# Values' product of a talking-heads attention: three bursts a half become twelve parts tied to visits

## The chip, the cores and the metric

The kernel runs on one core of a Trainium2 chip. The metric is the device time of that core in microseconds (us). The matrix engine is called PE here (its weight loads PEld), the vector engine DVE, the activation engine ACT, the general-purpose engine POOL; SP issues the DMAs.

## The reference

Attention with four batches, twelve heads, 448 rows and 64 elements a head, whose scores and whose softmax are both mixed over the heads, and two MLPs behind it:

```python
scores = scale * np.matmul(q, k.transpose(0, 1, 3, 2))
scores = np.einsum('bhij,hg->bgij', scores, w_pre)
attn = softmax(scores)                       # over j
attn = np.einsum('bhij,hg->bgij', attn, w_post)
x = np.matmul(attn, v)                       # heads side by side: 1792 x 768
h = x @ w_in;  x = (h * np.cos(h)) @ w_out   # 2048 wide
h = np.maximum(np.maximum(x @ w1, x @ w2), x @ w3)
return h @ w_out2
```

All of it is float32.

## The kernel before, in words

The rows of a batch are cut into *chunks* of 10, 11 or 12 *slots* of ten rows. For each chunk and each head pair `qk` (line 545) makes the scores in PSUM, `evac` copies them to SBUF and `send` (line 564) brings them by DMA into a grid in which the partitions hold rows and heads together; there are two grids. A *visit* is two slots of a chunk, 92 in all. For each visit `mix1` (line 568) mixes the scores over the heads, `rowmax`, `soft`, `guard`, `recip` and `wscale` do the softmax on DVE and ACT, `mix2` (line 606) mixes the result over the heads into PSUM banks of the pool `ps_t`, one for each slot, and `keep` (line 619) copies each of them into the tile `a2`.

One or two chunks form a *half* (`HALVES`, line 26; four batches of two halves of 220 and 230 columns). When all visits of a half are kept, `av` (line 631) multiplies them with the values: three steps a half, each of two head pairs, each of these a bank of `ps_t` and 16 matmuls in 8 groups, recorded as 32 in a step. `keepx` (line 643) copies each head pair's result out, one copy for each chunk, and `out` writes it to `xT` in HBM, from which the MLPs read.

Everything is put in order before the launch by a planner (`Plan`, line 372). Each step has a rank, a time on each engine that may do it, steps that it needs (`after`), steps that must be issued first (`behind`) and places that it takes and frees; the planner plays the engines through and issues the steps in the order that comes out, in which each engine then runs its queue. A rank counts blocks, two for each visit. The steps of the change stand at lines 675 to 725. The ranks of the first MLP work hang on `r0` (line 891), the start of the last chunk; `open_early` (line 914) needs the sends of the last chunk, `xget` (line 936) the outputs of a batch and a grid's place, and `open_late` (line 975) the last `keepx`.

PSUM has eight banks: three for `mix1` (`ps_m`), three of `ps_t`, two for `qk` (`ps_x`), which go to the MLPs later.

Of the kernel before, what the change touches and what calls it, by code (L numbers as in the profile page):

```python
# [9 lines left out]
F32 = mybir.dt.float32  # L10
# [6 lines left out]
B, H, S, D = 4, 12, 448, 64  # L17
# [4 lines left out]
RI = 10  # L22
JB, JC = 4, 112
IBLK = [(0, S)]
QG = 1
HALVES = [[[10, 12], [12, 11]]] * B
NHALF = 230
RT = 12
RH = RI // 2
BUFS = {"k": 10, "q": 9, "s": 8, "e": 5, "w2s": 3, "v": 7, "xs": 6, "a2": 2, "ps_m": 3, "ps_t": 3, "ps_x": 2}  # L30

RANK = {"fwget": 3.598, "fw": 2.0, "fwgap": 2.0, "fx": 3.474, "fxgap": 0.827, "x1": 2.568, "fh": 7.0, "fhgap": 0.483, "fa": 12.527}
WAIT = 0.034
# [410 lines left out]
def attention(ctx, tc, q, k, v, w_pre, w_post, same_row, xT, tp, mlps):  # L444
    nc = tc.nc
    scores_only = ctx.enter_context(ExitStack())
    pool = lambda n, b: ctx.enter_context(tc.tile_pool(name=n, bufs=b))
    psum = lambda n, b: ctx.enter_context(tc.tile_pool(name=n, bufs=b, space=bass.MemoryType.PSUM))
# [2 lines left out]
    ep, wp, st, const, vp, xp, ap_ = (  # L451
        pool("e", BUFS["e"]), pool("w2s", BUFS["w2s"]), pool("st", 8), pool("const", 1),
        pool("v", 1), pool("xs", BUFS["xs"]), pool("a2", BUFS["a2"]))
    ps_m, ps_t = (psum(n, BUFS[n]) for n in ("ps_m", "ps_t"))
    ps_x = scores_only.enter_context(
        tc.tile_pool(name="ps_x", bufs=BUFS["ps_x"], side="right", space=bass.MemoryType.PSUM))
    q = q.rearrange("(b c e i) -> b c e i", b=B, c=H // 2, e=4 * D)
# [22 lines left out]
    score, halves = [], []  # L480
    for b, sizes in enumerate(HALVES):
        i = 0
        for n, half in enumerate(sizes):
            start, column = i, 0
            for slots in half:
                i = min(i, S - RI * slots)
                score.append((b, i, RI * slots, slots, 2 * b + n, column))
# [140 lines left out]
    def pairs(x):  # L628
        return 2 * x, 2 * x + 1

    def av(half, x, _):
        b, _, _, m, _ = halves[half]
        a2 = live["a2", half]
        for hp in pairs(x):
            vt = live["v", b, hp]
            live["av", hp] = ps_t.tile([128, JB, H, RI], F32, name="aps")
            ps = live["av", hp] = live["av", hp].rearrange("p j g i -> p (j g i)")
            for j in range(JB):
                for g in range(2):
                    nc.tensor.matmul(ps[64 * g:64 * g + 64, :m], vt[:, j, g, :], a2[:, j, 2 * hp + g, :m],  # L640
                                     start=j == 0, stop=j == JB - 1)

    def keepx(half, hp, eng):

# [11 lines left out]

    before = {}

    def add(f, a, rank, engines, after=(), turn=False, **kw):

        key = f.__name__, *a
        plan.add(key, rank, partial(f, *a), engines, after, behind=before.get(f, ()) if turn else (), **kw)
        if turn:
            before[f] = [key]

    HP = H // 2


    for x in range(3):
# [5 lines left out]
    for n in range(NS):  # L675
        b = score[n][0]
        start, end = score[n - 1][0] != b or not n, n == NS - 1 or score[n + 1][0] != b
        for hp in range(HP):
            r = (first[n - 1] + 0.5 + 0.125 * score[n - 1][3] * hp) if n else -40.0 + hp
            if start:  # L680
                early = 8.0 if b else 20.0
                add(qget, (b, hp), r - early, {"D": 0.6}, turn=True, takes=["q"], lands=2.5)
                add(kget, (b, hp), r - early, {"D": 0.6}, turn=True, takes=["k"], lands=2.5)
            ring = score_bank(n, hp)[0]
            add(qk, (n, hp), r, {"T": 0.8}, [("qget", b, hp), ("kget", b, hp)], turn=True, takes=[ring] * 2,
                frees=[(f, (f + "get", b, hp)) for f in "kq"] if end else [])
            for h in range(2 * hp, 2 * hp + 2):
                add(evac, (n, h), r, {"A": 0.55, "V": 0.62}, [("qk", n, hp)], turn=True, takes=[place := copy_place(n, h)[0]], frees=[(ring, ("qk", n, hp), h % 2)])
                if h == 0:
                    plan.add(("new_t", n), r, lambda _: None, {}, [("evac", n, 0)], takes=["t"])  # L690
                add(send, (n, h), r, {"D": score[n][2] / 118.0}, [("evac", n, h), ("new_t", n)], turn=True, frees=[(place, ("evac", n, h))], lands=2.5)


    for y, (n, t, slots) in enumerate(visits):
        i = 2 * y
        key = lambda f, *x: (f, y, *x)
        add(mix1, (y,), i, {"T": 0.8}, [("wmix", 0), ("fill", n % 2)] + [("send", n, h) for h in range(H)], turn=True, takes=["ps_m"] * 2,
            frees=[("t", ("new_t", n))])
        for a in range(2):
# [6 lines left out]
            frees=[("e", key("soft", a)) for a in range(2)] + [("w2s", key("wscale"))])  # L706
        for c in slots:
            begin = n == halves[score[n][4]][4][0] and t == c == 0
            add(keep, (y, c), i + 1.5, {"A": 0.57, "V": 0.65}, [key("mix2")], turn=True, takes=["a2"] * begin,
                frees=[("ps_t", key("mix2"), c)])  # L710


    for half, (b, _, _, _, members) in enumerate(halves):
        last = (first + [N])[members[-1] + 1] - 1
        ends = [("keep", y, a) for y, x in enumerate(visits) if x[0] in members for a in x[2]]
        start = ends[0]
        for x in range(HP // 2):
            r = last + 2.5 + 3.0 * x
            for hp in pairs(x) if half % 2 == 0 else ():
                add(vget, (b, hp), r - 10.0, {"D": 0.8}, [("send", 0, H - 1)], turn=True, takes=["v"], lands=3.0)  # L720
            add(av, (half, x), r, {"T": 3.25}, [("vget", b, hp) for hp in pairs(x)] + ends, turn=True, takes=["ps_t"] * 2,
                frees=[("a2", start)] + [("v", ("vget", b, hp)) for hp in pairs(x) if half % 2])
            for hp in pairs(x):
                add(keepx, (half, hp), r, {"A": 0.45, "V": 0.5}, [("av", half, x)], turn=True, takes=["xs"], frees=[("ps_t", ("av", half, x), hp % 2)])
                add(out, (half, hp), r, {"D": 0.5}, [("keepx", half, hp)], turn=True, frees=[("xs", ("keepx", half, hp))], lands=3.0)


# [190 lines left out]
    for r, job in sorted(jobs):  # L918
        early = job[0] == "w" and job[1] < FG + 1
        if early:  # L920
            after = [("open_early",)]
# [11 lines left out]
        free(hold[0], ("convert", job, 6))  # L933
    for n in range(2):
        r = (r0, N - 1)[n] + RANK[("fx", "x1")[n]]
        add(xget, (n,), r, {"D": 3.6}, [("out", 2 * n + x, hp) for x in range(2) for hp in range(H // 2)] + [("xget", 0)] * n
            + [("block", FG)], takes=["t"])
        for c in range(KC):
            add(xhi, (n, c), r + 2.0 + c * RANK["fxgap"], {"A": 0.467}, [("xget", n)])
            add(xlo, (n, c), r + 2.0 + c * RANK["fxgap"], {"P": 1.09, "V": 0.535}, [("xhi", n, c)])  # L940
# [96 lines left out]
    for s in range(1, NSTEP):  # L1037
        if s == NSTEP - 1:
# [20 lines left out]
             behind=[("token", ("high", x, 0)) for x in ("11", "21", "T1", "T2", "T3", "T4")])  # L1059
# [35 lines left out]
    for u, (l, (j, wi)) in enumerate(units):  # L1095
# [8 lines left out]
        for i, (name, (eng, _, needs)) in enumerate(live["U", u][1].items()):  # L1104
            kind, x = name
# [109 lines left out]
```

## Time and profile before

| | |
|---|---|
| median of three runs | 1170.45 us (1168.78 to 1172.11) |
| the profiled execution | 1172.04 us |
| its span, first to last instruction | 1170.3 us |
| granted clock of PE, mean | 0.996 of full speed |
| attention, first mix1 to the last product's end | 23.3 to 387.9 us |

The profile is of one execution. Busy time of an engine is the time in which the profile shows an instruction in it; PE's matmuls are pipelined and their ends are modelled, so that PE can show as busy while it waits. A float32 matmul of the attention is recorded as two. The costs of PE work are therefore best read from start to start of groups that follow each other.

### The profile page before, as it was taken

To read this page: it belongs to the slowest core of one execution; us is meant where nothing else is said; L and a number is where in the kernel's file an instruction comes from. 1 tells how busy PE (TensorE), PEld (TensorE's weight loads), DVE (VectorE), ACT (ScalarE), POOL (GpSimd) and SP (SyncE) were. 2 spreads that over 40 slices of the span, in tenths; PEclk is the share of its full clock that TensorE was granted. 3 is DMA by queue.
4 is the path that set the end of the run, shared out by engine and by line. 5 is a ranking of instruction groups with operands and counts; after the bars stand their busy time and mean duration, and the time that the engine had idled before them with its cause. 6 is when DMAs were issued, how large, how long until landed. Compare 5 with 4: busy or idle time off the path is not lost.

```text
span 1170.3 us, 29431 instructions
## 1 busy us (share of the span) xinstructions
PE 1130.7 (97%) x11836; PEld 926.5 (79%) x11836; DVE 992.9 (85%) x2083; ACT 656.3 (56%) x1468; POOL 79.8 (7%) x69
## 2 busy tenths in 40 slices
PE   7899999899898899999999999999999999999998
PEld 2566566565556699999999999999999999999987
DVE  5878777777778899999999999997788679778994
ACT  3656556655657687555555555555534354445472
POOL 4000000000005110000000000000001021011110
PEclk9999999999999999999999999999999999999999
DMA  6785565645553655343434344431002221222233
GB/s 220 226 242 163 169 195 158 185 132 153 155 170 116 213 155 149 115 136 115 135 115 135 115 135 121 130 108 34 1 28 82 61 67 35 76 66 69 82 117 113
DMA packets 90696, 146.02 MB, mean 125 GB/s; under 512 B 8928, under 2 KB 73536, under 8 KB 90560
## 3 DMA queue, kind: packets, MB, share of 16 engines
q1 hardware_dynamic: 90304, 144.12, 40.8%
q8 instruction: 93, 1.52, 0.5%
q14 instruction: 43, 0.35, 0.1%
q0 software_dynamic: 256, 0.02, 0.0%
HBM read 84.96 MB, written 20.45 MB: 90 GB/s over the span
## 4 chain that ended last, share of the span: by engine, by line
PE 84%; DMA 6%; DVE 5%; issue 1%; ACT 1%; SPq 1%; ACTq 0%; DVEq 0%
PE ps L156 21%; PE ps L158 21%; PE ps L157 21%; PE mps L575 6%; PE aps L640 5%; PE aps L616 5%; PE ps L552 4%; DMA t<-s 3%; DMA x<-xT 1%; DVE nm L583 1%; DMA v<-in_v_dram 1%; DVE s L460 1%; DMA wraw<-in_w_in_dram 0%; ACT e L589 0%; DVE a L460 0%
## 5 line engine op out<-in xcount | busy, mean ns | idle before, releaser
L158 PE MATMUL ps<-x,w 128*128 128x448 f32 x816 | 300.0, 368 | 2.4 <-DVE x L147 1.5
L156 PE MATMUL ps<-x,w 128*128 128x448 f32 x816 | 300.4, 368 | 0.8 <-ACT gh L857 0.6
L157 PE MATMUL ps<-x,w 128*128 128x448 f32 x816 | 299.8, 367 | 0.5 <-DVE w L296 0.3
L156 PEld LDWEIGHTS ps<-x,w 128*128 128x128 f32 x816 | 153.7, 188 | 17.6 <-issue 2.4
L158 PEld LDWEIGHTS ps<-x,w 128*128 128x128 f32 x816 | 153.6, 188 | 17.4 <-POOL x L147 2.0
L157 PEld LDWEIGHTS ps<-x,w 128*128 128x128 f32 x816 | 153.7, 188 | 14.8 <-POOL w L131 0.8
L589 ACT ACTIVATE e<-mps,nm 128x448 f32<-128x448 f32 (+1 forms) x184 | 116.9, 637 | 79.2 <-DVE nm L583 59.3
L616 PEld LDWEIGHTS aps<-w2s,e 60*64 60x64 f32 x5760 | 108.7, 136 | 51.2 <-issue 23.8
L156 PE MATMUL ps<-gh,w 128*128 128x448 f32 x384 | 140.9, 367 | 0.0
L157 PE MATMUL ps<-gh,w 128*128 128x448 f32 x384 | 140.7, 366 | 0.0
L158 PE MATMUL ps<-gl,w 128*128 128x448 f32 x384 | 140.4, 366 | 0.0
L583 DVE TENSOR_REDUCE nm<-mps 128x1 f32<-128x448 f32 (+1 forms) x184 | 110.2, 616 | 30.8 <-PE mps L575 29.3
L293 ACT CAST w<-wf 128x384 fp32r<-128x384 f32 x168 | 81.1, 514 | 74.5 <-DVE wf L285 54.2
L616 PE MATMUL aps<-w2s,e 60*64 60x60 f32 x5760 | 112.7, 220 | 8.9 <-DVE w2s L603 6.2
L575 PE MATMUL mps<-t,w 64*64 64x448 f32 (+1 forms) x720 | 106.4, 558 | 10.2 <-DMA t<-s 6.2
L552 PE MATMUL ps<-k,q 64*64 64x448 f32 (+3 forms) x736 | 99.0, 551 | 5.1 <-ACT s L460 2.5
L814 DVE TENSOR_TENSOR acc<-ps,acc 128x448 f32<-128x448 f32 x168 | 100.2, 615 | 1.4 <-PE ps L158 1.4
L252 ACT ACTIVATE wf<-wraw 128x384 f32<-128x384 f32 x112 | 61.9, 553 | 51.3 <-DMA wraw<-in_w_out_dram 37.7
L296 DVE TENSOR_TENSOR w<-wf,w 128x384 fp32r<-128x384 f32 x132 | 73.7, 579 | 19.1 <-ACT w L293 18.3
L296 POOL TENSOR_TENSOR w<-wf,w 128x384 fp32r<-128x384 f32 x36 | 42.1, 1177 | 684.6 <-DVE wt L256 371.8
L640 PE MATMUL aps<-a,v 128*64 128x220 f32 (+1 forms) x768 | 78.0, 356 | 4.7 <-ACT xs L460 3.2
L640 PEld LDWEIGHTS aps<-a,v 128*64 128x64 f32 x768 | 54.2, 136 | 34.2 <-issue 5.9
(121 smaller groups left out, 1736.7 us busy)
## 6 DMA issues: line engine op xcount, KB each, us to landing
t<-s SPq DMA_DIRECT2D x96, 210.0 KB
wf<-w SPq DMA_DIRECT2D x96, 192.0 KB
wraw<-in_w_out_dram SPq DMA_DIRECT2D x44, 384.0 KB
wraw<-in_w_dram SPq DMA_DIRECT2D x36, 384.0 KB
wraw<-in_w_in_dram SPq DMA_DIRECT2D x32, 384.0 KB
t<-s SPq DMA_DIRECT2D x48, 192.5 KB
w<-wf SPq DMA_DIRECT2D x48, 192.0 KB
t<-s SPq DMA_DIRECT2D x43, 175.0 KB
```

The lines of the kernel that those rows point to most:

```text
L156: mm(w[0], x[0], start=first, stop=False)
L157: mm(w[1], x[0], start=False, stop=False)
L158: mm(w[0], x[1], start=False, stop=last)
L293: return nc.scalar.copy(A[x][0], w())
L296: return eng.tensor_sub(A[x][1], w(), f32(A[x][0]))
L552: nc.tensor.matmul(live["s", n, 2 * hp + g][r:end], live["q", b, hp][half, i0 + r:i0 + end], live["k", b, hp][half], start=True, stop=True)
L575: nc.tensor.matmul(live["m", v, a][64 * y:64 * y + 64], w1[k], grids[n % 2][k, t + y, :], start=True, stop=True)
L583: nc.vector.tensor_reduce(nm, of(v, live["m", v, a]), axis=AX.X, op=ALU.max, negate=True)
L589: nc.scalar.activation(of(v, e), of(v, live["m", v, a]), AF.Exp, bias=live["nm", v, a], scale=1.0, accum_out=live["z", v][:, a:a + 1])
L616: nc.tensor.matmul(live["a", v, y][64 * c:64 * c + 64, j, :, a, :], live["e", v, a][k, o:o + 64], live["w2s", v][k, a], start=True, stop=True)
L640: nc.tensor.matmul(ps[64 * g:64 * g + 64, :m], vt[:, j, g, :], a2[:, j, 2 * hp + g, :m], start=j == 0, stop=j == JB - 1)
L814: return nc.vector.tensor_add(acc, po, acc) if fg else nc.scalar.copy(acc, po)
```

## The change

`HALVES` gets a list for each batch: the first batch has halves of one chunk of 10 slots, one of 12, and two of 12 and 11; the last batch has 12 and 11, then 12, then 10 slots; the other two stay. The lists' chunks are in a new order in the last batch, and a half's number is counted as the halves are made.

`ps_t` has two banks instead of three, and a pool `ps_v` of one bank takes both head pairs of a step of `av`, side by side. A step of `av` becomes four parts: for each of the two head pairs, chunks 0 and 1 of the four in which the keys lie, then chunks 2 and 3, 4 matmuls each (8 recorded). The twelve parts of a half are issued behind the `mix1` of visits: the first behind that of the second visit after the half's last one, the rest spread over as many visits as the next half has, at most twelve. Parts whose visit would lie behind the last one are not tied. `keepx` follows the last part of its own head pair. `qk` of a chunk is issued behind `mix1` of a visit of the chunk before, from two visits ahead of that chunk's start for the first two head pairs to two visits into it for the sixth.

Values are loaded for the half that starts a batch, as before, and freed by the half that ends one; `xget` needs the outputs of all halves of its batch.

```diff
-HALVES = [[[10, 12], [12, 11]]] * B
+HALVES = [[[10], [12], [12, 11]], [[10, 12], [12, 11]], [[10, 12], [12, 11]], [[12, 11], [12], [10]]]
-BUFS = {..., "ps_m": 3, "ps_t": 3, "ps_x": 2}
+BUFS = {..., "ps_m": 3, "ps_t": 2, "ps_v": 1, "ps_x": 2}
...
-    def av(half, x, _):
+    def av(half, x, y, _):
         b, _, _, m, _ = halves[half]
         a2 = live["a2", half]
-        for hp in pairs(x):
-            vt = live["v", b, hp]
-            live["av", hp] = ps_t.tile([128, JB, H, RI], F32, name="aps")
-            ps = live["av", hp] = live["av", hp].rearrange("p j g i -> p (j g i)")
-            for j in range(JB):
-                for g in range(2):
-                    nc.tensor.matmul(ps[64 * g:64 * g + 64, :m], vt[:, j, g, :], a2[:, j, 2 * hp + g, :m],
-                                     start=j == 0, stop=j == JB - 1)
+        if y == 0:
+            both = ps_v.tile([128, 2 * NHALF], F32, name="avps")
+            for n, hp in enumerate(pairs(x)):
+                live["av", hp] = both[:, n * NHALF:(n + 1) * NHALF]
+        hp = pairs(x)[y // 2]
+        for j in range(2 * (y % 2), 2 * (y % 2) + 2):
+            for g in range(2):
+                nc.tensor.matmul(live["av", hp][64 * g:64 * g + 64, :m], live["v", b, hp][:, j, g, :], a2[:, j, 2 * hp + g, :m],
+                                 start=j == 0, stop=j == JB - 1)
...
+    starts = [next(y for y, x in enumerate(visits) if x[0] == n) for n in range(NS)] + [len(visits)]
+
+    def from_visit(y):
+        return [("mix1", y)] if 0 <= y < len(visits) else []
...
             add(qk, (n, hp), r, {"T": 0.8}, [("qget", b, hp), ("kget", b, hp)], turn=True, takes=[ring] * 2,
+                behind=from_visit(starts[n - 1] - 2 + max(hp - 1, 0)) if n > 1 else [],
                 frees=[(f, (f + "get", b, hp)) for f in "kq"] if end else [])
...
+        ylast = starts[members[-1] + 1] - 1
+        room = min(12, starts[halves[half + 1][4][-1] + 1] - 1 - ylast) if half + 1 < len(halves) else 12
...
-            add(av, (half, x), r, {"T": 3.25}, [("vget", b, hp) for hp in pairs(x)] + ends, turn=True, takes=["ps_t"] * 2,
-                frees=[("a2", start)] + [("v", ("vget", b, hp)) for hp in pairs(x) if half % 2])
+            for y in range(4):
+                add(av, (half, x, y), r + 0.75 * y, {"T": 0.05 + 0.0034 * halves[half][3]}, behind=from_visit(ylast + 2 + (4 * x + y) * room // 12), after= [("vget", b, hp) for hp in pairs(x)] + ends, turn=True, takes=["ps_v"] * (y == 0),
+                    frees=[("a2", start)] * (y == 3) + [("v", ("vget", b, hp)) for hp in pairs(x) if halves[half][1] + halves[half][2] == S and y == 3])
             for hp in pairs(x):
-                add(keepx, (half, hp), r, {"A": 0.45, "V": 0.5}, [("av", half, x)], turn=True, takes=["xs"], frees=[("ps_t", ("av", half, x), hp % 2)])
+                add(keepx, (half, hp), r, {"A": 0.45, "V": 0.5}, [("av", half, x, 1 + 2 * (hp % 2))], turn=True, takes=["xs"], frees=[("ps_v", ("av", half, x, 0))])
...
-        add(xget, (n,), r, {"D": 3.6}, [("out", 2 * n + x, hp) for x in range(2) for hp in range(H // 2)] + [("xget", 0)] * n
+        add(xget, (n,), r, {"D": 3.6}, [("out", x, hp) for x, y in enumerate(halves) if y[0] == n for hp in range(H // 2)] + [("xget", 0)] * n
             + [("block", FG)], takes=["t"])
```

## Rows read from the trace of the kernel before

**Rows 1.** The page's first part: engine, busy us, share of the span, instructions.

```profile
PE 1130.7 (97%) x11836; PEld 926.5 (79%) x11836; DVE 992.9 (85%) x2083; ACT 656.3 (56%) x1468; POOL 79.8 (7%) x69
```

**Rows 2.** PE's timeline: start and length in us, line, operation; a gapless piece.

```profile
196.56 0.96 PE L575 MATMUL mps<-t,w 64*64 64x448 f32 x8
197.45 3.33 PE L640 MATMUL aps<-a,v 128*64 128x230 f32 x32
200.71 0.98 PE L552 MATMUL ps<-k,q 64*64 64x448 f32 x8
201.51 1.10 PE L616 MATMUL aps<-w2s,e 60*64 60x60 f32 x64
202.44 0.93 PE L575 MATMUL mps<-t,w 64*64 64x448 f32 x8
203.19 0.93 PE L552 MATMUL ps<-k,q 64*64 64x448 f32 x8
203.95 1.10 PE L616 MATMUL aps<-w2s,e 60*64 60x60 f32 x64
```

**Rows 3.** The same view, a product burst of 220 columns.

```profile
70.69 1.02 PE L575 MATMUL mps<-t,w 64*64 64x448 f32 x8
71.64 3.19 PE L640 MATMUL aps<-a,v 128*64 128x220 f32 x32
74.76 0.98 PE L575 MATMUL mps<-t,w 64*64 64x448 f32 x8
```

**Rows 4.** The page's costliest groups: line, tile, shape, count, busy, mean ns, idle before.

```profile
L616 PE MATMUL aps<-w2s,e 60*64 60x60 f32 x5760 | 112.7, 220 | 8.9 <-DVE w2s L603 6.2
L575 PE MATMUL mps<-t,w 64*64 64x448 f32 (+1 forms) x720 | 106.4, 558 | 10.2 <-DMA t<-s 6.2
...
L640 PE MATMUL aps<-a,v 128*64 128x220 f32 (+1 forms) x768 | 78.0, 356 | 4.7 <-ACT xs L460 3.2
```

**Rows 5.** PE's timeline, the first mix1.

```profile
23.31 0.98 PE L575 MATMUL mps<-t,w 64*64 64x448 f32 x8 [0.54 <-DMA t<-s]
```

**Rows 6.** PE's timeline, the last product and the MLP matmuls behind it.

```profile
375.05 4.88 PE L640 MATMUL aps<-a,v 128*64 128x230 f32 x48 [0.84 <-DVE a L460]
383.09 4.88 PE L640 MATMUL aps<-a,v 128*64 128x230 f32 x48 [3.16 <-ACT xs L460]
387.90 0.47 PE L156 MATMUL ps<-x,w 128*128 128x448 f32 x1
```

**Rows 7.** All engines in 25 us of the MLPs: PE, PEld, DVE, ACT, POOL, clock, DMA.

```profile
450.00:475.00 25.00, 25.00 (x124) 23.02 (x124) 24.09 (x50) 15.89 (x32) 0.00 (x0) 1.00 0.51 148
```

**Rows 8.** Two stretches, mix1 alone (L575): length, busy us and count on PE, PEld.

```profile
190.80:211.30 20.50, 3.83 (x32) 0.99 (x32) 1.00 0.62 186
211.30:235.50 24.20, 8.84 (x64) 2.75 (x64) 1.00 0.61 180
```

**Rows 9.** The first of these stretches, values' product alone (L640), same columns.

```profile
190.80:211.30 20.50, 9.98 (x96) 6.63 (x96) 1.00 0.62 186
```

**Rows 10.** The head, mix1 alone (L575), same columns.

```profile
23.30:65.00 41.70, 17.73 (x112) 5.31 (x112) 1.00 0.74 224
```

**Rows 11.** The head, mix2 alone (L616), same columns.

```profile
23.30:65.00 41.70, 15.39 (x768) 14.47 (x768) 1.00 0.74 224
```

**Rows 12.** The head, qk alone (L552), same columns.

```profile
23.30:65.00 41.70, 14.37 (x112) 4.57 (x112) 1.00 0.74 224
```

**Rows 13.** The last visits, all engines: PE, PEld, DVE, ACT, POOL, clock, DMA.

```profile
327.00:375.00 48.00, 43.16 (x938) 27.96 (x936) 40.27 (x96) 31.47 (x79) 10.87 (x9) 0.96 0.51 157
```

**Rows 14.** The timeline of ACT and DVE: copies out of PSUM.

```profile
200.82 0.59 DVE L460 COPY xs<-aps 128x120 f32<-128x120 f32 x2 [0.50 <-PE aps L640]
...
202.65 0.57 ACT L460 COPY a<-aps 128x480 f32<-128x480 f32 x1 [0.38 <-PE aps L616]
202.71 0.66 DVE L460 COPY a<-aps 128x480 f32<-128x480 f32 x1 [0.30 <-PE aps L616]
```

**Rows 15.** Who waited for whom: us in total, times, longest.

```profile
PE mps L575 <- DMA t<-s: 6.2, 7, 1.6
```

More of the change, by code (lines that the diff above doesn't have):

```diff
@@ L29 @@
 RH = RI // 2
-BUFS = {"k": 10, "q": 9, "s": 8, "e": 5, "w2s": 3, "v": 7, "xs": 6, "a2": 2, "ps_m": 3, "ps_t": 3, "ps_x": 2}
+BUFS = {"k": 10, "q": 9, "s": 8, "e": 5, "w2s": 3, "v": 7, "xs": 6, "a2": 2, "ps_m": 3, "ps_t": 2, "ps_v": 1, "ps_x": 2}
 RANK = {"fwget": 3.598, "fw": 2.0, "fwgap": 2.0, "fx": 3.474, "fxgap": 0.827, "x1": 2.568, "fh": 7.0, "fhgap": 0.483, "fa": 12.527}
@@ L453, in attention @@
         pool("v", 1), pool("xs", BUFS["xs"]), pool("a2", BUFS["a2"]))
-    ps_m, ps_t = (psum(n, BUFS[n]) for n in ("ps_m", "ps_t"))
+    ps_m, ps_t, ps_v = (psum(n, BUFS[n]) for n in ("ps_m", "ps_t", "ps_v"))
     ps_x = scores_only.enter_context(
@@ L483, in attention @@
         for n, half in enumerate(sizes):
-            start, column = i, 0
+            start, column, nhalf = min(i, S - RI * half[0]), 0, len(halves)
             for slots in half:
                 i = min(i, S - RI * slots)
-                score.append((b, i, RI * slots, slots, 2 * b + n, column))
+                score.append((b, i, RI * slots, slots, nhalf, column))
                 column += RI * slots
@@ L657, in attention, with add @@
     before = {}
-    def add(f, a, rank, engines, after=(), turn=False, **kw):
+    def add(f, a, rank, engines, after=(), turn=False, behind=(), **kw):
         key = f.__name__, *a
-        plan.add(key, rank, partial(f, *a), engines, after, behind=before.get(f, ()) if turn else (), **kw)
+        plan.add(key, rank, partial(f, *a), engines, after, behind=list(before.get(f, ()) if turn else ()) + list(behind), **kw)
         if turn:
@@ L718, in attention @@
             r = last + 2.5 + 3.0 * x
-            for hp in pairs(x) if half % 2 == 0 else ():
+            for hp in pairs(x) if halves[half][1] == 0 else ():
                 add(vget, (b, hp), r - 10.0, {"D": 0.8}, [("send", 0, H - 1)], turn=True, takes=["v"], lands=3.0)
-            add(av, (half, x), r, {"T": 3.25}, [("vget", b, hp) for hp in pairs(x)] + ends, turn=True, takes=["ps_t"] * 2,
-                frees=[("a2", start)] + [("v", ("vget", b, hp)) for hp in pairs(x) if half % 2])
+            for y in range(4):
+                add(av, (half, x, y), r + 0.75 * y, {"T": 0.05 + 0.0034 * halves[half][3]}, behind=from_visit(ylast + 2 + (4 * x + y) * room // 12), after= [("vget", b, hp) for hp in pairs(x)] + ends, turn=True, takes=["ps_v"] * (y == 0),
+                    frees=[("a2", start)] * (y == 3) + [("v", ("vget", b, hp)) for hp in pairs(x) if halves[half][1] + halves[half][2] == S and y == 3])
             for hp in pairs(x):
-                add(keepx, (half, hp), r, {"A": 0.45, "V": 0.5}, [("av", half, x)], turn=True, takes=["xs"], frees=[("ps_t", ("av", half, x), hp % 2)])
+                add(keepx, (half, hp), r, {"A": 0.45, "V": 0.5}, [("av", half, x, 1 + 2 * (hp % 2))], turn=True, takes=["xs"], frees=[("ps_v", ("av", half, x, 0))])
                 add(out, (half, hp), r, {"D": 0.5}, [("keepx", half, hp)], turn=True, frees=[("xs", ("keepx", half, hp))], lands=3.0)
```

## Prediction

> **What bounds the kernel now.** I read the engine lines of the page first [rows 1]: PE is busy for 97% of the span, DVE for 85%. A busy PE is not yet a full one, so the next thing to read is the price of each kind of PE work when nothing holds it, from a stretch in which PE's rows follow each other without a gap [rows 2]. From start to start, the next group begins 0.75 us after a mix1 or qk of 8 recorded matmuls, 0.93 us after a mix2 of 64, 3.26 us after 32 of values' product at 230 columns and 3.12 us at 220 [rows 3]. With the counts of the page [rows 4] the attention, from the first mix1 at 23.31 us [rows 5] to the first matmul of the MLPs behind the last product, 387.90 us [rows 6], costs PE: mix1 720/8 x 0.75 = 67.5; mix2 5760/64 x 0.93 = 83.7; qk 16 chunks x 6 head pairs less the ten groups that run ahead of 23.31, 86 x 0.75 = 64.5; the product 24 bursts, 12 x 3.26 + 12 x 3.12 = 76.6; MLP matmuls that slip in before 373 us, 36 x 0.2 (25 us for 124 in [rows 7]) = 7.3. Entering the product costs extra: mix1 to product takes 0.89 us in rows 2 and 0.95 us in rows 3 where mix1 to another group takes 0.75, and the group behind the product takes 0.80 instead of 0.75. I call that 0.2 us a burst, 22 separate bursts, 4.4 us. The sum is 304 us out of 387.9 - 23.3 = 364.6. So some 60 us of the attention are gaps on PE, though PE shows as busy in most of them, because the modelled ends of pipelined matmuls cover short waits.
>
> Where the gaps lie, two neighbouring stretches show [rows 8]. From 190.8 to 211.3 us there are four visits (32/8) and three product bursts (96/32) [rows 9]: 20.5 - 3 x 3.26 = 10.7 us, 2.7 us a visit for the rest, against 0.75 + 0.75 + 0.93 = 2.44 of work. From 211.3 to 235.5 us there are eight visits and no product: 3.03 us a visit, so 0.59 us waited in each. While the product runs, the others catch up and PE is full; behind it PE waits for softmax, copies and, at chunk borders, for sends. Soon after 413 us PE runs its matmuls back to back [rows 7], and nothing of this change reaches there: what counts is when the MLPs come into their full pace.
>
> **The change part by part.**
> *Product in parts.* Each burst of 32 becomes four parts of 8. At 230 columns a part costs 3.26/4 = 0.81 us. Ten stretches instead of eight give 960 recorded matmuls instead of 768; the columns stay. Between 220 and 230 columns the price of one grows by (3.26 - 3.12)/32 = 4.4 ns for 10 columns, which leaves about 6 ns of fixed cost in each, so the 192 more cost some 1.2 us. The switches grow: the stretches have 100, 120, 230, 220, 230, 220, 230, 230, 120 and 100 columns; nine of them are spread over 6, 12, 11, 12, 11, 12, 12, 6 and 5 visits and the tenth is a tail of about three groups, some 90 groups instead of 22: 68 x 0.2 = 13.6 us more PE work. Ends of this price: 0 where a part falls into a wait that is there anyway, 0.25 us each (0.95 - 0.75 and the 0.05 behind it) = 17 us. I take 13.6, and 15 us with the fixed cost.
>
> *Tied to visits.* Against that stand the gaps. With a part in each visit PE needs 2.47 (qk are 96 to 92 visits) + 0.8 + 0.2 = 3.47 us a visit, while the other engines get through a visit in 3.03 at the latest; PE is then the slower side everywhere, as it is now in the product stretches, where it waits about 0.1 us a visit. I take 0.2 us for the 76 visits between head and end: 15 us, where now 32 us lie (60 less 9.5 at the head and 19 at the end). Both ends: 0.1 would make 8 us, 0.59 as without product 45 us.
>
> *Three stretches in the first batch.* The head, 23.31 to 65 us, now holds no product: 112/8 = 14 mix1, 768/64 = 12 mix2 and 112/8 = 14 qk [rows 10 to 12] make 32 us out of 41.7, 9.5 us of gaps. The 100 column stretch, about 4.4 us and six switches, now runs there from the seventh visit. I take 6 us of gaps left. Its price if nothing is hidden: the values of batch 0 load six visits earlier, twelve more DMAs on SP ahead of the sends of the second chunk; a late chunk costs one visit, 3.5 us.
>
> *Three in the last batch.* Now 96 matmuls of 230 columns stand behind the last visit: 375.05 to 379.93, a wait for a copy until 383.09, and again until 387.90 [rows 6]: 12.9 us. Behind the change 96 of 100 columns stand there, each about 100 x 0.44 + 6 = 50 ns, 4.8 us, and what is left of the 120 columns. The 230 columns before run in visits in which PE waits anyway because weight conversions fill DVE, 84% busy from 327 to 375 us [rows 13]. So PE reaches the end of the product some 7 us sooner, gaps 19 to 12. The x and weight work of the MLPs on DVE is then late next; I let a part of this gain go below.
>
> *Banks.* ps_t falls from three to two. The two copies of mix2's output start 0.21 and 0.27 us behind it and end 0.93 us behind it [rows 14], and the next mix2 comes 1.51 us behind, so two buffers hold at this pace: cost 0. If each second copy were held by one more DVE operation (0.66 us) it would be 92 x 0.1 = 9 us; on the gain side the product no longer takes two of the three from mix2, whose start at 201.51 us lies right behind the end of the xs copies at 201.41; at most one such copy, 0.57 us, a burst, 14 us. I take 0 as the rows of copies are nearest. The product's own single bank is reused after its two copies; a copy of 0.27 us x 2 and its handover lie within the 3.5 us between two parts: 0. Behind a waiting matmul the whole of PE's queue waits, mix1 of the next visit first, so this cover matters (second rival).
>
> *qk tied, ranks, outputs.* qk are only kept from going early; sends still have four visits, 14 us, for copies and landing: 0, between -6 and +6 us, all that mix1 now waits for sends [rows 15] gone or doubled. The MLP weights' ranks hang on the start of the last chunk, which is now five visits before the end: 0, up to 3.5 us either way. The 12 more output DMAs go through SP with time to spare; the output copies keep their number.
>
> *Sum.* Gaps 60 to 15 + 6 + 12 = 33, PE work 15 more: 60 - 33 - 15 = 12 us sooner, all in front of 413 us. The profiled execution takes 1172.04 us, 1.7 beyond its span and 1.6 above the median of the runs: 1172 - 12 = 1160, as a median 1158 us.
>
> **Rivals.**
> *The switches eat it (slower side).* The gaps may be latency and landing waits at chunk borders, where no part is to hand because the next ones are tied behind the very mix1 that waits. Then the 15 us of added PE work are paid and the gaps fall by less. It decides below 15 of 60 us closed; with 8 closed the time is 1170 + 7 = 1177. For it: mix1 waits for sends seven times now, and 0.14 to 0.2 us at each entry are in the rows. Against it: 32 us of the gaps lie in the middle, and only 6.2 us of them name a send.
> The Trainium skill, TensorEngine Tiling (Array Packing), Key Properties, says that changing the tiling mode drains the engine; mix1, mix2 and qk use 64-row tiles and the product 128-row ones, and the trace agrees with a drain at each entry.
>
> *The shared bank makes PE wait.* Both head pairs of a burst lie in one bank, and if its copies and matmuls take turns, each third part waits for the even pair's copy, each first for the odd pair's: 60 places. One costs up to 0.2 + 0.57 + 0.2 = 1 us when the copy is not done. One in five exposed gives 12 us: 1170. For it: DVE and ACT work through their queues in order, and copies stand behind 0.6 us operations. Against it: a visit lies between the parts.
> The Trainium skill, PSUM — Partial Sum Buffer, PSUM bank collisions raise a hardware error, wants two engines kept off one bank and quadrant even at other columns; no row here shows such a pair.
>
> *The MLPs do not start sooner.* DVE's conversions and the loads of x set 413 us; of the 12 us only the middle's part arrives, less a visit of later ranks: 1164 to 1168.
>
> *All gaps close.* With 0.1 us a visit and mix2 freed from the product's buffers the gaps fall to 20: 1146.
>
> **How the numbers follow.** Forecast 0.5 (own range 1150 to 1166), all gaps close 0.12, MLPs late 0.08, shared bank 0.1, switches 0.2. The range, 1140 to 1177, leaves out about one tenth on either side: the upper half of the switches' case, and a pace with hardly a gap. A measurement of this kernel tells 0.3%, 3.5 us, from no change: faster takes the forecast, the closing case and a little over half of the third, 0.67; same takes the rest of the third, most of the bank's case at its given price and a bit of the switches', 0.12; slower takes the rest, 0.21.
>
> **What would show it.** The windows of the middle should hold 0.2 us of gap a visit and an even 3.5 to 3.7 us from mix1 to mix1, no more stretches of 5.1 beside stretches of 3.0. The product's line should have 960 matmuls in some 90 groups; mix1 or qk before a part should still take 0.9. The last product should end near 375 us and the first dense MLP stretch begin near 400. Wrong would be: parts that wait for ACT or DVE xs, mix2 waiting for its copies over 0.3 us a visit, sends waited for by more than 12 us in all, or PE idle between the last product and 413.

## The result, and the profile after

The changed kernel takes 1175.73 us (median of 20 runs) against 1169.89 us for the kernel before on the same chip: 1.0054 of its time, 95% interval 1.0037 to 1.0072. It is slower by about 6 us where 12 us less were forecast. The profiled execution took 1174.96 us, its span is 1173.2.

The page of the changed kernel, the lines that answer to [rows 1, 4] (the product is line L641 now):

```profile
PE 1136.6 (97%) x12028; PEld 912.8 (78%) x12028; DVE 989.2 (84%) x2075; ACT 667.3 (57%) x1476; POOL 79.0 (7%) x69
...
L616 PE MATMUL aps<-w2s,e 60*64 60x60 f32 x5760 | 109.4, 223 | 7.7 <-DVE w2s L603 3.9
...
L575 PE MATMUL mps<-t,w 64*64 64x448 f32 (+1 forms) x720 | 93.2, 554 | 14.4 <-DMA t<-s 7.7
...
L641 PE MATMUL avps<-a,v 128*64 128x230 f32 (+3 forms) x960 | 96.2, 331 | 3.0 <-DVE xs L460 2.2
```

The product has its 960 matmuls, in 93 groups of PE's order (22 before; the expectations below count one or two more). PE is busy 6 us longer. Mix1 waits more (14.4 us for 10.2). Sends make 7.7 us of that (6.2 before), and 4.6 us are put down to loads of K and V; mix1 reads neither, and both waits stand at the first visit of a chunk (visits 40 and 51), where what it needs are the sends. The waits of PE, us in total, times, longest, answer to [rows 15]:

```profile
PE mps L575 <- DMA t<-s: 7.7, 6, 2.3
PE aps L616 <- DVE w2s L603: 3.9, 4, 2.9
PE mps L575 <- DMA k<-in_k_dram: 2.9, 1, 2.9
...
PE avps L641 <- DVE xs L460: 2.2, 1, 2.2
PE mps L575 <- DMA v<-in_v_dram: 1.7, 1, 1.7
```

PE's timeline in the middle (start, length, line, operation), the answer to [rows 2]:

```profile
274.89 1.16 PE L616 MATMUL aps<-w2s,e 60*64 60x60 f32 x64
275.86 0.93 PE L552 MATMUL ps<-k,q 64*64 64x448 f32 x8
276.62 0.93 PE L575 MATMUL mps<-t,w 64*64 64x448 f32 x8
277.48 0.96 PE L641 MATMUL avps<-a,v 128*64 128x220 f32 x8
278.38 1.16 PE L616 MATMUL aps<-w2s,e 60*64 60x60 f32 x64
279.35 0.93 PE L552 MATMUL ps<-k,q 64*64 64x448 f32 x8
280.11 0.93 PE L575 MATMUL mps<-t,w 64*64 64x448 f32 x4
```

Here the forecast's picture holds: mix1 to mix1 takes 280.11 - 276.62 = 3.49 us with no gap in it. The loss lies elsewhere. In the table are the starts of mix1 of some visits, and the start of the last matmul of the product, in one profiled execution of each kernel: for the kernel before in us, for the others as the lag behind it.

| kernel | visit 0 | 5 | 11 | 17 | 40 | 81 | product's end |
|---|---|---|---|---|---|---|---|
| before | 23.3 | 38.7 | 57.3 | 78.4 | 168.6 | 323.0 | 387.6 |
| changed | +0.3 | +4.5 | +9.0 | +9.8 | +7.4 | +7.5 | +6.2 |
| late_notie | -2.0 | -2.9 | -1.2 | +0.1 | +1.1 | +1.4 | -0.3 |
| before_tie | +1.2 | -0.2 | +6.3 | +10.6 | +7.9 | +6.7 | +6.8 |
| before_tied | +5.1 | +8.1 | +9.5 | +11.7 | +8.6 | +3.2 | +2.5 |
| own_three | -0.3 | +0.5 | +1.0 | +5.9 | +8.1 | +16.3 | +16.9 |
| late_notie_threet | +1.2 | +1.3 | +3.2 | +2.5 | -1.5 | -6.7 | -7.7 |

The changed kernel is 9.0 us late at visit 11 and 9.8 us at visit 17, and gets back 3.6 us from there to the product's end. Some 4 us of the lag at visit 11 are product that only comes earlier: five groups of 16 matmuls, 0.84 us each, have run by then and none in the kernel before. By visit 17 both have done about as many columns (14400 and 14080). Visits 17 to 81 take 242.3 us for 244.5. (Most runs of one kernel lie within 6 us of their median, so I read from this table only steps of several us, and totals from the medians. The traced execution of before_tied is its longest, 1174.83 us, 11.5 above its median, so its first columns are no measure of that kernel; the only trace of late_values is of an execution of 3876 us and is not read here.) Its first visits, the answer to [rows 5], the start of a chunk in the middle (visit 40), and the end, the answer to [rows 6], on PE's timeline:

```profile
23.64 0.98 PE L575 MATMUL mps<-t,w 64*64 64x448 f32 x8 [0.87 <-DMA t<-s]
...
33.34 1.98 PE L616 MATMUL aps<-w2s,e 60*64 60x60 f32 x64 [2.88 <-DVE w2s L603]
...
43.21 1.76 PE L575 MATMUL mps<-t,w 64*64 64x448 f32 x8 [2.31 <-DMA t<-s]
44.68 2.00 PE L616 MATMUL aps<-w2s,e 60*64 60x60 f32 x64
...
172.10 0.99 PE L552 MATMUL ps<-k,q 64*64 64x448 f32 x8
176.00 1.44 PE L575 MATMUL mps<-t,w 64*64 64x448 f32 x8 [2.92 <-DMA k<-in_k_dram]
...
385.41 1.59 PE L641 MATMUL avps<-a,v 128*64 128x100 f32 x32
387.52 1.59 PE L641 MATMUL avps<-a,v 128*64 128x100 f32 x32 [0.51 <-ACT xs L460]
391.34 2.89 PE L641 MATMUL avps<-a,v 128*64 128x100 f32 x32 [2.23 <-DVE xs L460]
394.16 0.74 PE L156 MATMUL ps<-x,w 128*128 128x448 f32 x1
```

Why visit 5 is late stands in SP's own queue. Kernel before (start, length, what it issues, how many):

```profile
18.38 12.49 SPq L566 DMA_DIRECT2D t<-s  x14
30.97 3.36 SPq L537 DMA_DIRECT2D v<-in_v_dram  x6
...
49.40 1.65 SPq L566 DMA_DIRECT2D t<-s  x2
```

(The last row is the end of chunk 2's sends.) Changed kernel, the 14 sends of the first row:

```profile
18.37 4.17 SPq L566 DMA_DIRECT2D t<-s  x5
22.64 2.19 SPq L537 DMA_DIRECT2D v<-in_v_dram  x4
24.92 4.38 SPq L566 DMA_DIRECT2D t<-s  x5
29.36 2.33 SPq L537 DMA_DIRECT2D v<-in_v_dram  x4
31.79 4.82 SPq L566 DMA_DIRECT2D t<-s  x4
```

The last of chunk 1's sends is out at 36.6 us in place of 30.9, because eight of V's DMAs stand between them.

### The profile page after: what moved, and what is told of

Read it like the earlier page. It is cut to its first block, busy times and chain, and to the rows that moved or that the text cites. A ratio compares the mean times of both kernels' runs of the same rounds, so it can differ in the third digit from the quotient of the medians.

```text
span 1173.2 us, 29906 instructions
## 1 busy us (share of the span) xinstructions
PE 1136.6 (97%) x12028; PEld 912.8 (78%) x12028; DVE 989.2 (84%) x2075; ACT 667.3 (57%) x1476; POOL 79.0 (7%) x69
## 4 chain that ended last, share of the span: by engine, by line
PE 88%; DVE 4%; DMA 4%; issue 1%; ACT 1%; SPq 0%; POOL 0%; DVEq 0%; ACTq 0%
PE ps L156 21%; PE ps L157 21%; PE ps L158 21%; PE aps L616 7%; PE avps L641 6%; PE mps L575 6%; PE ps L552 5%; DMA t<-s 2%; DVE nm L583 1%; DVE wf L268 0%; DVE wt L264 0%; DVE a L460 0%; DMA k<-in_k_dram 0%; DMA v<-in_v_dram 0%; DVE wt L260 0%
## 5 line engine op out<-in xcount | busy, mean ns | idle before, releaser
L616 PEld LDWEIGHTS aps<-w2s,e 60*64 60x64 f32 x5760 | 99.9, 137 | 43.0 <-issue 23.6
L616 PE MATMUL aps<-w2s,e 60*64 60x60 f32 x5760 | 109.4, 223 | 7.7 <-DVE w2s L603 3.9
L641 PEld LDWEIGHTS avps<-a,v 128*64 128x64 f32 x960 | 55.1, 139 | 69.8 <-issue 28.6
L575 PE MATMUL mps<-t,w 64*64 64x448 f32 (+1 forms) x720 | 93.2, 554 | 14.4 <-DMA t<-s 7.7
L641 PE MATMUL avps<-a,v 128*64 128x230 f32 (+3 forms) x960 | 96.2, 331 | 3.0 <-DVE xs L460 2.2
L552 PE MATMUL ps<-k,q 64*64 64x448 f32 (+3 forms) x736 | 93.2, 554 | 3.5 <-ACT s L460 2.0
L460 DVE COPY a<-aps 128x480 f32<-128x480 f32 x87 | 57.1, 657 | 37.1 <-PE aps L616 36.9
```

Of the source, the lines that this page charges most:

```text
L552: nc.tensor.matmul(live["s", n, 2 * hp + g][r:end], live["q", b, hp][half, i0 + r:i0 + end], live["k", b, hp][half], start=True, stop=True)
L575: nc.tensor.matmul(live["m", v, a][64 * y:64 * y + 64], w1[k], grids[n % 2][k, t + y, :], start=True, stop=True)
L616: nc.tensor.matmul(live["a", v, y][64 * c:64 * c + 64, j, :, a, :], live["e", v, a][k, o:o + 64], live["w2s", v][k, a], start=True, stop=True)
L641: nc.tensor.matmul(live["av", hp][64 * g:64 * g + 64, :m], live["v", b, hp][:, j, g, :], a2[:, j, 2 * hp + g, :m], start=j == 0, stop=j == ...
```

## Experiments

Each ratio is to the kernel before in the same set of runs, with its 95% interval.

**First set: one part undone at a time.** *late_values*, the changed kernel with V's loads of the first batch twelve ranks later:

```diff
-                add(vget, (b, hp), r - 10.0, ...
+                add(vget, (b, hp), r - 10.0 + 12.0 * (b == 0), ...
```

> The changed kernel with one number altered: the loads of the first batch's values get the rank they had before, so that SP issues them behind the twelve sends of the second chunk and not after the third. Theory 'loads' (the 9 to 10 us by which the changed kernel lags at its 11th visit come from these loads standing ahead of the sends): mix1 of the sixth visit starts near 39 us instead of 43.2, the lag at the 11th visit falls from +10.8 to under +3, the time falls by 6 to 9 us, to about 1167 to 1169. Rival 'qk tie' (PE has nothing to do at 30 us because the third chunk's qk are held back): lag and time stay within 2 us. Rival 'switches in the head': the same, within 2 us.

*no_qk_tie*, without the tie of qk:

```diff
-                behind=from_visit(starts[n - 1] - 2 + max(hp - 1, 0)) if n > 1 else [],
```

> The changed kernel without the tie of qk to visits. Theory 'loads': the lag at the 11th visit stays at 8 us or more, since SP's order of loads and sends is the same; the time moves by less than 3 us. Rival 'qk tie': qk fills the gap of 2.9 us at 30 us again, the lag falls under 4 us and the time by 5 us or more.

*first_whole*, with the first batch in two halves:

```diff
-HALVES = [[[10], [12], [12, 11]], ...
+HALVES = [[[10, 12], [12, 11]], ...
```

> The changed kernel with the first batch in two halves as before (10 and 12, 12 and 11 slots). Both the loads and the early parts of the head go. Theory 'loads': about the time of the kernel with late loads, 1167 to 1170, as the parts of the first stretches save little. If the early parts themselves cost, it is faster than that kernel by 2 us or more; if they fill the head's waits, slower by 2 us or more.

*six_parts*, one part for each head pair:

```diff
-        hp = pairs(x)[y // 2]
-        for j in range(2 * (y % 2), 2 * (y % 2) + 2):
+        hp = pairs(x)[y]
+        for j in range(JB):
```

> The changed kernel with six parts a half instead of twelve, each a whole head pair (16 recorded matmuls), tied to every second visit of those before; bank, ties and halves stay. Theory 'switch price' (each entry into the product and exit from it costs PE about 0.27 us, and in the middle PE has no other waits left): some 45 switches fewer, 45 x 0.27 = 12 us at most, I expect 5 to 12 us off, most of it from 64 to 365 us. Rival 'the gaps come back' (only a part in each visit keeps PE busy): the middle stays within 2 us or gets slower.

Measured: late_values 1177.13 us, 1.0057 (1.0027 to 1.0088); no_qk_tie 1174.99, 1.0042 (1.0019 to 1.0066); first_whole 1183.31, 1.0119 (1.0080 to 1.0157); six_parts 1175.14, 1.0042 (1.0016 to 1.0068). No single part gives the loss back; late_values and six_parts missed what their first theory expected. Without the tie the lag is still 8.9 us at visit 17. Two halves in the first batch make it worse: visit 5 is then only 0.8 us late, but visit 17 is 13.9 us late. I take from this that two things hold up the head, one after the other, and that whichever is left keeps most of the lag; the next set tests it.

**Second set: the head.** *late_notie* has both edits of late_values and no_qk_tie; *late_notie_six* has six parts besides.

> The changed kernel with two of its side effects taken out together: V's loads of the first batch stand behind all twelve sends of chunk 1 again, and qk's tie to a visit is gone. The first batch keeps its three stretches, the product its parts and its bank. If the loss is made in the first ten visits by both acting through one queue (each alone left it: 1.0057 and 1.0042 of the kernel before), the lag against the kernel before is at most 3 us at visit 10 and at visit 17 (8 to 10 in the changed kernel), and the time is 1165 to 1169, 6 to 9 under the changed kernel. If the loss is the price of more parts and more switches, wherever they lie, it stays at 1174 to 1177.

> The same with six parts a half in place of twelve (a part is one head pair). Against the run beside it, the two middle batches lose 23 switches. At 0.2 us of switch a part, as forecast, and 0.3, as the traces of six parts and of twelve lie apart, all four batches win 7 to 12 us if visits are bound by TensorE throughout, and nothing if what the parts free is waited for elsewhere (the median of six parts stood only 0.6 below the changed kernel): 1158 to 1163 by the first, 1165 to 1169 by the second.

*before_tie* is the kernel before with the qk tie alone:

```diff
+                behind=from_visit(starts[n - 1] - 2 + max(hp - 1, 0)) if n > 1 else [],
```

> The kernel before with one edit: qk of every chunk from 2 on tied to the visit two before the chunk's start, one more for each head pair. If the tie moves chunk 2's sends behind the loads of Q and K of batch 1, the lag is 4 us or more by visit 17 and the time 4 to 8 us above the kernel before. If the tie is free, as forecast, it stays within 2 us.

*before_early_v* is the kernel before with V's loads earlier:

```diff
-                add(vget, (b, hp), r - 10.0, ...
+                add(vget, (b, hp), r - 10.0 - 12.0 * (b == 0), ...
```

> The kernel before with one edit: V's loads of the first batch stand some sends earlier in SP's queue, after the third of chunk 1. If they hold up chunk 1's last sends, visits 3 to 5 start 3 to 5 us later and the time is 2 to 5 us above the kernel before. If a late chunk costs one visit of 3.5 us at most and is made up later, it stays within 2 us.

Measured: late_notie 1169.96, 1.0013 (0.9986 to 1.0040); late_notie_six 1169.14, 0.9995 (0.9965 to 1.0025); before_tie 1177.24, 1.0059 (1.0031 to 1.0086); before_early_v 1172.21, 1.0014 (0.9987 to 1.0041). With both edits the lag at visit 17 is gone (+0.1 us) and 0.0041, 5 us, of the loss with it. The tie alone makes a loss as large as the whole change's; early loads alone make none that can be told. PE's timeline of before_tie shows the place, the start of chunk 2 (visit 11):

```profile
55.42 1.18 PE L552 MATMUL ps<-k,q 64*64 64x448 f32 x8
63.53 1.77 PE L575 MATMUL mps<-t,w 64*64 64x448 f32 x8 [6.93 <-DMA t<-s]
65.05 1.95 PE L616 MATMUL aps<-w2s,e 60*64 60x60 f32 x64
```

and SP's queue shows why: chunk 2's last four sends go out in pairs between the loads of Q and K of batch 1.

```profile
49.47 0.38 SPq L531 DMA_DIRECT2D q<-in_q_dram  x1
49.89 1.47 SPq L527 DMA_DIRECT2D k<-in_k_dram  x1
51.46 1.65 SPq L566 DMA_DIRECT2D t<-s  x2
53.17 0.51 SPq L531 DMA_DIRECT2D q<-in_q_dram  x1
54.56 0.88 SPq L527 DMA_DIRECT2D k<-in_k_dram  x1
55.54 1.65 SPq L566 DMA_DIRECT2D t<-s  x2
```

In the kernel before, chunk 2's last send is issued by 51.1 us (the row at 49.40 above), ahead of those loads; here by 57.2. In both, mix1 of visit 11 starts some 6.3 us later (57.3 and 63.5): what the last send is late, the visit is late.

**Third set: why nothing is left of the 12 us.** late_notie stands level with the kernel before. These runs have its two edits, and vary stretches and parts. *late_notie_whole* has two halves in every batch, *whole_six* six parts in them, *whole_three* three; *late_notie_three* has three parts with the changed kernel's stretches.

```diff
-HALVES = [[[10], [12], [12, 11]], [[10, 12], [12, 11]], [[10, 12], [12, 11]], [[12, 11], [12], [10]]]
+HALVES = [[[10, 12], [12, 11]]] * 4
```

and for three parts

```diff
-            for y in range(4):
-                add(av, (half, x, y), ...
+            for y in range(1):
+                add(av, (half, x, y), ... behind=from_visit(ylast + 2 + 4 * x * room // 12), ...
```

where `av` then does both head pairs of a step in the one part.

> The changed kernel without the qk tie, with V's loads of the first batch behind chunk 1's sends, and with two halves in every batch as in the kernel before. What is left of the change: the product in twelve parts a half tied to visits (82 groups on TensorE in place of 23), and a bank of its own. If the third stretch at the first and at the last batch is what ends the product early and pays, this stands 3 to 8 us above the run with it (1170.0): 1173 to 1178. If the third stretches bring nothing, it is 1168 to 1171; fewer groups (82 for 95) would then take off 3 at 0.25 us each.

> As the run beside it, with six parts a half (44 groups in place of 82). At 0.25 us a group, as the middles of six parts and of twelve lie apart in the traces (23 groups, 5.8 us), 38 groups take off 9 us: 1160 to 1163. If what a group frees is waited for at the next chunk's sends, the time falls by 2 or less: 1167 to 1170.

> As the run beside it, with three parts a half (23 groups, as many as in the kernel before): of the change only the tie of the parts to visits and the bank of its own are left. If the tie and the bank close gaps as forecast and only the groups' price ate it, this is the fastest: 1153 to 1160. If the gaps close because the parts are small, or if the waits that go come back as waits for sends, it stands at the kernel before's 1167 to 1172.

> Three parts a half (30 groups in place of 95) and the third stretches in the first and last batch as in the changed kernel; no qk tie, V's loads late. Against 1170.0 with twelve parts: 0.25 us for 65 groups would take off 16 (1152 to 1157); if the groups' price is hidden or returns as waits, 1166 to 1171.

Measured: late_notie_whole 1190.91, 1.0187 (1.0158 to 1.0216); whole_six 1172.25, 1.0041 (1.0020 to 1.0062); whole_three 1187.03, 1.0171 (1.0134 to 1.0208); late_notie_three 1184.96, 1.0142 (1.0108 to 1.0176). All four runs fell outside every range that I had given them. From twelve parts to three the kernel gets 15 us slower with the changed kernel's stretches and 4 us faster with two halves, and six parts are best in both; and with twelve the third stretches were worth 21 us where I gave them 8 at most. So in this bank the price of groups, which falls with each of these steps, does not decide by itself: what fewer groups give back is lost elsewhere. whole_three differs from the kernel before mainly in the tie of its parts and in the banks.

**Fourth and fifth set: tie or bank.** *before_tied* is the kernel before with its three parts tied, and three ps_t banks as before:

```diff
-            add(av, (half, x), r, {"T": 3.25}, ..., takes=["ps_t"] * 2,
+            add(av, (half, x), r, {"T": 3.25}, ..., takes=["ps_t"] * 2, behind=from_visit(ylast + 2 + 4 * x * room // 12),
```

> The kernel before (three ps_t banks, the product in them, 23 groups) with one edit: the three parts of a half tied to visits four apart. If the bank of its own is what made three tied parts slow (1187.0, 18 above the kernel before), this stays at 1168 to 1173. If the tie itself made them slow, it is at 1180 to 1188.

*before_six* cuts its parts in two (38 groups), *before_six_tied* ties these too:

```diff
+            for y, hp in enumerate(pairs(x)):
+                add(av, (half, x, y), r + 1.5 * y, {"T": 1.6}, ..., takes=["ps_t"], ...
```

> The kernel before with one edit: each part of the product cut into its two head pairs, so that a part takes one ps_t bank for 1.6 us in place of two for 3.2 (39 groups for 23). If smaller parts close gaps by more than the 0.25 us that a group costs, 1160 to 1167; if the waits that go come back as waits for sends, 1168 to 1172.

> The same, with the six parts tied to visits two apart (44 groups). Against whole_six, which has the parts in a bank of its own (1172.3, 3.7 above the kernel before): if the bank costs also with small parts, this is 5 to 10 us faster, 1162 to 1167; if small parts make the third ps_t bank needless, within 2 us of it, 1170 to 1174.

*late_notie_sixt* is late_notie_six, *late_notie_threet* late_notie_three, both without the bank of its own; *own_three* is before_tied with it.

```diff
-"ps_t": 2, "ps_v": 1,
+"ps_t": 3,
...
-            both = ps_v.tile([128, 2 * NHALF], F32, name="avps")
+            live["av", hp] = ps_t.tile([128, JB, H, RI], F32, name="aps").rearrange("p j g i -> p (j g i)")
```

> The changed kernel without the qk tie and with V late, six parts a half, in the ps_t banks (three) in place of a bank of its own. Against 1169.1 for the same in a bank of its own: 1162 to 1166 if the third ps_t bank counts, 1168 to 1171 if not.

> before_tied with one edit: the product in a bank of its own, and two ps_t banks left in place of three. V's loads stand where they stand in before_tied. If the bank makes the difference, 1180 to 1188; if V's later place made it in the earlier three-part run, 1162 to 1168.

> The three tied parts in three ps_t banks, with the third stretches in the first and last batch (29 groups), V late, no qk tie. If the third stretches still pay at the end (the product of late_notie_sixt ended at 376.4 in its trace, 11 before the kernel before's), 1156 to 1162; if they are worth nothing beside the tie, 1162 to 1166, as before_tied (1163.4).

Measured: before_tied 1163.35, 0.9969 (0.9944 to 0.9994); before_six 1185.93, 1.0164 (1.0138 to 1.0191); before_six_tied 1168.74, 1.0004 (0.9986 to 1.0022); late_notie_sixt 1163.08, 0.9962 (0.9939 to 0.9985); own_three 1188.72, 1.0150 (1.0124 to 1.0177); late_notie_threet 1161.17, 0.9919 (0.9895 to 0.9942).

before_tied came out faster than either range, before_six slower, before_six_tied between its two. Untied, six parts lose 0.0164; tied, nothing: here the tie itself is worth 0.016, 19 us.

before_tied and own_three differ in the bank: 1.0150 - 0.9969 = 0.018, 21 us. late_notie_three and late_notie_threet differ in it as well: 0.022, 26 us. With six parts (late_notie_six, late_notie_sixt) it is 0.0033, 4 us, with intervals that overlap. V's place, which differed in the earlier three-part run, is out of it. (The edit does two things at once: mix2 keeps two banks of three, and both head pairs of the product share one where each had its own. The runs do not part them.) The same piece of the middle on PE's timeline, own_three first:

```profile
203.91 1.70 PE L575 MATMUL mps<-t,w 64*64 64x448 f32 x8
205.54 3.33 PE L641 MATMUL avps<-a,v 128*64 128x230 f32 x32
208.80 1.16 PE L616 MATMUL aps<-w2s,e 60*64 60x60 f32 x64
...
212.97 1.83 PE L552 MATMUL ps<-k,q 64*64 64x448 f32 x8
```

and before_tied:

```profile
211.50 1.69 PE L575 MATMUL mps<-t,w 64*64 64x448 f32 x8
213.12 3.33 PE L640 MATMUL aps<-a,v 128*64 128x230 f32 x32
216.38 0.98 PE L552 MATMUL ps<-k,q 64*64 64x448 f32 x8
217.18 1.10 PE L616 MATMUL aps<-w2s,e 60*64 60x60 f32 x64
```

No bank is waited for in so many words. What changes is the order that the planner writes: from visit 17 to 81, the product is followed by mix2 at once in 14 of own_three's 16 groups, and by qk or mix1 in all 16 of before_tied's; late_notie_three and late_notie_threet show the same 14 and 0 of 16. As I read it, the softmax wait is then covered by the product, but the next qk comes later, and PE stalls inside groups: qk of eight matmuls takes 1.83 us in the row above, 0.93 without a stall. Summed over the starts of matmuls in this stretch, PE spends 40.3 us inside qk groups against 30.8, 37.6 against 32.6 inside mix1 groups, and 18.1 against 3.9 from a qk to the mix1 behind it; other steps are 10 us shorter, and the stretch takes 254.9 us against 236.1. In own_three the profile names 6.8 us of waits of mix1 for sends there, in before_tied none (2.8 us for other DMAs). That the order is what costs is argued from these two traces; no run changes it alone, and why the planner's order turns on the third bank was not taken further.

late_notie_threet beats both kernels, by 0.0081 and, across the sets, by some 0.0135. Its profile gives the price of the parts too (busy us, mean ns of one, idle before):

```profile
L575 PE MATMUL mps<-t,w 64*64 64x448 f32 (+1 forms) x720 | 107.7, 559 | 7.4 <-DMA t<-s 6.8 <-ACT e L589 0.6
...
L638 PE MATMUL aps<-a,v 128*64 128x230 f32 (+3 forms) x960 | 82.3, 328 | 3.1 <-DVE a L460 3.1
```

The same 960 matmuls keep PE busy for 82.3 us in 28 groups and for 96.2 in the changed kernel's 93: 13.9/65 = 0.21 us a group. Mix1 waits 7.4 us in place of 14.4. With three ps_t banks the price of groups shows in the time: from six parts to three (55 and 28 groups) it falls by 0.0043, 5 us, for 27 groups fewer, and from before_six_tied to before_tied by 0.0035, 4 us, for 21; the intervals of each two touch, but both falls are what the groups cost at 0.2.

Left open: why the third stretches are worth 0.017 with twelve parts in a bank of their own and 0.003 to 0.005 with three or six; why before_six, cut but not tied, is 0.016 slower; and the changed kernel's twelve parts with three ps_t banks, which weren't tried. So what the bank costs the changed kernel itself is not shown.

## Why the prediction was wrong

**The step that failed is the sum of the gaps, "Gaps 60 to 15 + 6 + 12 = 33".** I counted the traces again with the prediction's own prices: 0.75 and 0.93 us a group, the product by its columns, 0.2 us for each of its groups and for each MLP matmul. The added work is 14 us, near the 15 forecast. But the gaps fall from 60.7 us only to 52.2: 8.5 us closed where 27 were forecast.

| gaps of PE, us, in one execution | before | changed | late_notie | forecast |
|---|---|---|---|---|
| first mix1 to visit 17 | 9.8 | 17.2 | 9.7 | 9.5 to 6 |
| visit 17 to 81 | 34.0 | 24.0 | 27.5 | 32 to 15 |
| visit 81 to the first matmul behind the product | 16.9 | 11.0 | 10.7 | 19 to 12 |
| all | 60.7 | 52.2 | 47.9 | 60 to 33 |

(The forecast's borders lie a little differently, and before_tie and before_early_v, whose product is as in the kernel before, have 29.4 and 31.0 in the middle; read steps of several us only.)

In the middle the even pace came inside the chunks: 27 of 64 steps from mix1 to mix1 take 3.4 to 3.7 us. But of the ten that take over 4.8 us, nine lead into the first visit of a chunk. These nine last 57.2 us, 26 more than nine steps of 3.5, and that is about all that is left of the middle's gaps. Each of these visits starts 2.8 to 5.6 us behind the issue of its chunk's last send, and no part may fill the wait, as the next ones are tied to this visit or a later one (the row at 176.00 above). So the term of 0.2 us for each visit left out the wait for sends at chunk borders.

In the head, the term of 6 us became 17.2, and 9.7 without the tie of qk and the early loads. Here, and at the banks, **edits were costed at nothing or nearly so** that the runs price:
- *Banks, "cost 0".* The cover named, a mix2 every 1.51 us behind copies of 0.93, is real: mix2 hardly ever starts behind a copy that has just ended (2 of 93 pieces in own_three's middle, 7 of 71 in the changed kernel's, within 0.2 us). But giving the product a bank of its own cost 21 to 26 us with the product in three parts and some 4 with six, with another written order. For three parts the upper bound of 9 us was too low; for the twelve of the change no run shows the cost. The rival on the shared bank does not show where it was expected; waits of a part for xs are named at the end alone, 0.51 and 2.23 us.
- *qk tied, "sends still have four visits, 14 us".* The tie alone costs 0.0059, 7 us (4 to 10), about the upper edge of the six us either way. Four visits were there, but I counted only copies and landing. Sends leave through SP in order, and the tie put the loads of Q and K of the next batch in among them.
- *V's loads "ahead of the sends": at most one visit, 3.5 us.* They cost 0.0014 alone, not to be told from none. In the changed kernel visit 5 is 4.5 us late with them (3.4 without the tie, 0.8 in first_whole, where they load later), and taking them out together with the tie gives back 0.0041, 5 us, and the 7.5 us of gaps in the head.

**The mechanism was right in part.** Tying the product to visits closes gaps: before_tied does it with no other edit and wins 0.0031, 4 us (1 to 7), and its middle falls from 244.5 to 236.1 us (240.7 and 241.6 in before_tie and before_early_v, where the product is not tied). With six parts the tie is worth 0.016. Three tied parts with the third stretches and with neither of the two side effects nor the bank win 0.0081, 9.5 us, against 12 forecast; that this comes near the forecast is partly luck, as it has 28 groups and not the 93 of the change.

**The price of a switch was right in size.** 0.2 us was taken; the busy time gives 0.21. The rows of the middle give 277.48 - 276.62 - 0.75 = 0.11 before a part, 278.38 - 277.48 less a fourth of 3.12 = 0.12 inside it, and 0.04 in the mix2 behind: 0.27 us. The Trainium skill, TensorEngine Tiling (Array Packing), Key Properties, says that changing the tiling mode drains the engine; the trace agrees, with this price at each part. Over 71 more groups that is 15 to 19 us. (The fixed cost of a matmul, on the other hand, was a slip: 3.26 us/32 less 230 columns at 0.44 ns leaves 1 ns and not 6, so that the 192 more cost 0.2 us and not 1.2.)

**The rival "the switches eat it"** had both its condition and its sum in the trace: no part to hand at chunk borders, and "with 8 closed the time is 1170 + 7 = 1177", where 8.5 closed and the median is 1176. In late_notie 13 us close against 15 paid, and it stands level with the kernel before. It is not the whole story: 7.5 us of the missing gain are the head's, which it did not name, and with three parts in the same bank the switches go and the kernel is slower still.

**The signs.** 960 matmuls in some 90 groups and mix1 before a part at 0.9 came as forecast; an even 3.5 us a visit came inside the chunks only, and the mean from visit 17 to 81 is 3.8. The product's end at 375 did not: 394.2. Of the 7 us forecast at the end, 2 came: from visit 91 (364.0 and 372.3) to the first matmul behind the product it takes 21.9 us instead of 23.9, as the three pieces of 100 columns wait for each other's copies. The MLPs behind got 3.4 us shorter (span less that matmul's start: 782.4 and 779.0), which is why the profiled execution lost 2.9 us and not 6.

## What to carry to other kernels

An edit that only reorders work is not free because its engine has time: list the queue that each moved instruction goes through, here SP's, and what then stands ahead of it. Where a planner writes the order, giving up a buffer can change that order and cost time although no row shows a wait for that buffer; test it by itself. Work that is tied behind a step cannot fill the wait of that step: look at the borders, here the first visit of a chunk, and not at the mean gap. When a change bundles a good idea with its props, try the idea alone first: three tied parts were faster than twelve in a bank of their own.

## What the runs showed of the hardware

A gap on PE was paid for twice. The windows of before_tie (length, PE busy, granted clock, DMA share, GB/s):

```profile
56.00:63.00 7.00, 0.60 (x7) 0.90 0.85 226
63.00:68.00 5.00, 4.47 (x80) 0.50 0.81 199
68.00:75.00 7.00, 6.88 (x178) 0.97 0.59 175
```

After seven microseconds with 0.60 busy, the granted clock was 0.50, the level of 1.2 GHz, for the next five, and mix2 of 64 took 1.95 us in place of 1.10. The changed kernel's head shows it after waits of 2.88 and 2.31 us: the mean granted clock is 0.66 from 33 to 38 us and from 43 to 48 us, with mix2 at 1.98 and 2.00 us. The Trainium skill, TensorE: Matmul & The Clock Gate, Part 1 (The HAM clock gate), says that the gate follows how busy the engine has lately been; the trace agrees (0.60 us busy in seven, then 0.50). The second payment is, as an estimate, half of those five microseconds, 2.5 us, and the prediction had no term for it.
